# Attention with six head slots in place of five, loads a unit ahead, shared tail tiles and an earlier division of the last unit but one

## The chip, the cores and the metric

The kernel runs on one core of one Trainium2 chip. The metric is the device time of one execution in microseconds (us); the time given for a kernel is the median of its runs.

## The reference

The input `x` (2048 tokens, 576 wide) is layer-normed. Branch A is sliding-window attention with 32 heads of width 18 and a window of 256 keys; branch B is a gated MLP whose gate mixes tokens with a 2048 x 2048 matrix. The output is `x + A * silu(B)`.

```python
xn = layernorm(x)
q, k, v = heads(xn @ wqkv)                        # 32 heads of 18
p = softmax(where(0 <= i - j < 256, q @ k.T * 18**-0.5, -1e9))
s = merge(p @ v) @ wo
z = gelu(xn @ w_in); z1, z2 = z[:, :2304], layernorm(z[:, 2304:])
g = silu((z1 * (w_sp @ z2 + b_sp[:, None])) @ w_out)
out = x + s * g
```

## The kernel before

Products are formed in float32r with each operand split into a high and a low part (`hi, lo`), so that one product is three matmuls. The stages follow each other: q and k (stored in DRAM as `st_d`), v, z2, then **attention, with the z1 projection laid in between**, then the product with `wo` (L1148, tiles `wops`), then the token mixing (L1389) and the output (L1482).

**Attention.** A unit is four heads and one half of the tokens: `UNITS` holds 16 of them, units 0 to 7 for the first half and 8 to 15 for the second. A unit's heads come in two pairs; pair `p` is unit `p // 2`, heads `2a` and `2a + 1` with `a = p % 2`. A pair lies in one *slot*, a tile `att0` to `att4` of 128 x 2304 (q in the first 1024 columns, k behind it), the two heads in partitions 0 to 63 and 64 to 127. Pair `p` uses slot `p % NSLOT` (`q_of`, `k_of`). In orders without buffer numbers the slots read `att_2227` (slot 0), `att_2228` (1), `att_2229` (2), `att_6846` (3), `att_6848` (4) and, after the change, `att_6850` (5).

- `pair_jobs` (L547) loads a pair by eight DMAs from `st_d`. `open_unit(u)` puts the loads of pairs `2u + 3` and `2u + 4` on the planner's clock, 400 ns apart, as soon as all scores of unit `u - 1` have been handed out.
- `max_item` (L597 on TensorE, tile `sp`; L601 on VectorE) finds each query's maximum; 32 items make a unit. `max_split` and `max_end` (L610 to L623) split and turn the maxima, and four small DMAs `att<-mhl` (L627) put them into rows 54 and 55 of the slots.
- `scores` (L721, tile `tps`) makes scores less maximum, ScalarE takes the exponential (L725, `pt<-tps`), GpSimd clears what lies outside the band (L733, L736), and `pv` multiplies with v (L749, tile `ops`, a single PSUM buffer). v comes with a column of ones, so that each head's sum comes out as a row too.
- After half of a unit, and after the whole, ScalarE moves `ops` into `ou` (L764). There are two `ou` buffers: unit `u` writes into the one of unit `u - 2`, after that unit's stores `o_d<-ou` (L800). The last unit has a tile of its own, `oul`.
- `finish(u)` sets the division: `den<-ou` (L811), reciprocal (L784) at `INVERT_AT`, through DRAM (`r_d`, L786) back as `rp` (L791) at `FETCH_AT`, four multiplications on GpSimd (L795) and four stores (L800) at the times of `DIVIDE_AT`, counted from the end of the unit. For the last unit the same steps stand in the list `last` and run in the stage behind.
- `z1_rows(r)` is the fill: 972 matmuls for each half of the array (rows 0 to 63 write `ma`, rows 64 to 127 write `mb`, L668), 54 to a block of 128 features. `load_z1` fetches a block's weights into `z1raw` (L637), one buffer. A block's weights are fetched when the half that is behind enters the block before, and split on ScalarE and GpSimd (L683, `z1wh`, `z1wl`) from when *either* half is in the second bank of that block before.

**What sets the order.** A planner in the kernel keeps a clock per half of the array, with a fixed cost for each operation, and hands out at each step a score, a maximum, a fill matmul or a batch of `pv`. A maximum may be handed out when the planner's clock has passed the pair's last load by `LOAD_NS` (5500). All DMAs are issued by SyncE (SP), whose queue runs in the order that the planner gives; so do the queues of the four engines.

**Behind attention**, `wo_load(t)` loads 256 tokens of the heads' output from `o_d` (L973, L975; `t % 3` chooses `spare`, slot 0 or slot 1), `wo_split` (L1134 on ScalarE, L1135 and L1136 on VectorE) splits them into `ohl0`, `ohl1`, `ohl2`, and two halves of 28 matmuls (L1148) each make 128 tokens, moved out as `so` (L1181). `ohl0` lies where the `ou` and `rp` buffers of attention were.

Of the kernel before, what the change touches and what calls it, by code (L numbers as in the profile page):

```python
# [9 lines left out]
F32 = mybir.dt.float32  # L10
# [6 lines left out]
P = 128  # L17
# [19 lines left out]
NSLOT = 5  # L37
# [8 lines left out]
KEEP_NS = 1200  # L46
INVERT_AT = 9000
# [10 lines left out]
def f32(ap):  # L58
    return ap.bitcast(F32)
# [3 lines left out]
def kernel(  # L63
# [169 lines left out]
    with ExitStack() as early:  # L233
# [283 lines left out]
        with ExitStack() as ph:  # L517
# [37 lines left out]
            def after(ns, fn):  # L555
                waiting.append((clock + ns, fn))
# [182 lines left out]
            def pv(u, kb, qa, qz):  # L739
# [17 lines left out]
                if kb == 4 * c + 3:  # L757
                    if c % 2 == 0:
                        while parts.get(u - 2):
                            part(u - 2)  # L760
                        ous[u] = (ap_.tile([P, HS], F32, name="ou", bufs=2) if u < NU - 1 else
                                  aa.tile([P, HS], F32, name="oul", bufs=1))
                    ou = ous[u]
                    act.activation(ou[:, c % 2 * 512:c % 2 * 512 + 512], o_ps.pop(c), AF.Copy)  # L764
                    free_at = use("act", 500, 120)
                    for t in later:
                        t[0] = free_at
                    if c % 2 == 1:
                        finish(u, ou)
# [7 lines left out]
            def finish(u, ou):  # L777
# [5 lines left out]
                def invert():  # L783
                    dve.reciprocal(den, den)  # L784
                    t = use("dve", 270) - clock + 300
                    after(t + 1500, lambda: sp.dma_start(r_d[u].rearrange("h (a b) -> (h a) b", b=HS // 32), den))  # L786
                    for i in range(4):
                        after(t + FETCH_AT + 400 * i, partial(sums, i))
# [21 lines left out]
                else:  # L810
                    after(busy["act"] - clock + 1000, lambda: sp.dma_start(den, ou[DH::32, :]))  # L811
                    after(INVERT_AT, invert)
                    parts[u] = [partial(divide, a) for a in range(4)] + [partial(store, i) for i in range(4)]
                    for ns in DIVIDE_AT:
                        after(ns, partial(part, u))
# [153 lines left out]
            def wo_load(t):  # L969
                ts_ = slice(t * 2 * P, (t + 1) * 2 * P)  # L970
                home = (spare, slots[0], slots[1])[t % 3]
                raw = f32(home[:, :10 * P]).rearrange("p (k c) -> p k c", k=5)
# [3 lines left out]
                return raw  # L976

# [13 lines left out]
            spare = ab.tile([P, 10 * P], F32R, name="spare")  # L991
            with ExitStack() as heads:
# [22 lines left out]
                def open_unit(u):  # L1015

                    jobs = [(p, it) for p in (2 * u + 3, 2 * u + 4) if p < 2 * NU for it in [pair_jobs(p)]
                            for _ in range(8)]
                    for i, (p, it) in enumerate(jobs):
                        ns = 300 + 400 * i + (4000 if u == 0 else 0)  # L1020
# [538 lines left out]
```

## Time and profile before

| | us |
|---|---|
| median of 3 runs (1927.2 to 1933.6) | 1932.25 |
| the profiled execution | 1929.15 |
| its span | 1927.4 |
| attention with the fill | about 428 to 935 of the span |
| product with `wo` | about 942 to 1003 |

The span runs from the first to the last instruction; 1.75 us of the execution lie around it. PE is TensorE's matmuls, PEld its weight loads, DVE VectorE, ACT ScalarE, POOL GpSimd; SPq is SyncE, which issues the DMAs. PEclk is the share of TensorE's full clock that was granted. In a row of a timeline, what stands in brackets is the idle time before the instruction and what ended it.

### The profile page before, as it was taken

How to read it: one execution, taken by the hardware profiler on the slowest of the kernel's cores; microseconds unless marked ns; L12 is line 12 of the kernel's file. 1: busy time of each engine (PE TensorE's matmuls, PEld its weight loads, DVE VectorE, ACT ScalarE, POOL GpSimd, SP SyncE). 2: the span in 40 equal slices, each digit the busy share in tenths (PEclk: the TensorE clock that was granted, in tenths of full speed). 3: DMA queues.
4: the chain of work that ended last, by engine and by line, in shares of the span. 5: the costliest groups of instructions: out<-in, count | busy, mean ns of one | idle time of the engine just before them, and what ended most of it. 6: DMA issues, size and time to landing. Idle time of an engine off the chain costs nothing.

```text
span 1927.4 us, 38537 instructions
## 1 busy us (share of the span) xinstructions
PE 1867.1 (97%) x14552; PEld 1619.2 (84%) x14552; DVE 1037.9 (54%) x2273; ACT 916.3 (48%) x1760; POOL 397.8 (21%) x486
## 2 busy tenths in 40 slices
PE   8999999999988999999899999999999999999999
PEld 8999999997666676677698888888888888899998
DVE  6320334466666555654227787747776667563222
ACT  5432223225565555666458575465554534442211
POOL 3232343343445454455200000000000000000000
PEclk9999999999999998999899999999999999999999
DMA  8895798875565555664678677766676656875441
GB/s 259 196 235 150 240 316 274 272 256 156 154 167 160 156 164 151 155 181 132 176 246 274 218 256 243 248 211 225 201 255 225 193 162 190 270 230 157 141 139 58
DMA packets 234314, 389.85 MB, mean 202 GB/s; under 512 B 51984, under 2 KB 145680, under 8 KB 234000
## 3 DMA queue, kind: packets, MB, share of 16 engines
q1 hardware_dynamic: 234128, 387.39, 65.2%
q8 instruction: 114, 1.87, 0.4%
q14 instruction: 72, 0.59, 0.1%
HBM read 274.74 MB, written 111.78 MB: 201 GB/s over the span
## 4 chain that ended last, share of the span: by engine, by line
PE 76%; DMA 11%; DVE 5%; SPq 4%; issue 2%; ACT 2%; POOL 0%; POOLq 0%; DVEq 0%; ACTq 0%
PE acc L1389 32%; PE po L1482 12%; PE mb L204 9%; PE ma L204 5%; PE ma L668 4%; DMA att<-st_d 3%; PE ops L749 3%; PE mb L668 3%; PE tps L721 2%; PE sp L597 2%; PE wops L1148 2%; SPq L360 2%; DMA z1raw<-in_w_z_dram 2%; DMA st_d<-qkhl 1%; DMA rp<-r_d 1%
## 5 line engine op out<-in xcount | busy, mean ns | idle before, releaser
L1389 PE MATMUL acc<-spl,zh 128*128 128x512 f32 x1008 | 392.6, 390 | 0.9 <-DVE spl L114 0.5
L1389 PE MATMUL acc<-sph,zh 128*128 128x512 f32 x1008 | 392.2, 389 | 0.0
L1389 PE MATMUL acc<-sph,zl 128*128 128x512 f32 x1008 | 392.2, 389 | 0.0
L601 DVE CUSTOM_DVE_ANT_0 junk<-sp,band 128x384 bf16<-128x384 f32 (+1 forms) x512 | 276.3, 540 | 187.3 <-PE sp L597 101.3
L725 ACT ACTIVATE pt<-tps 128x384 f32<-128x384 f32 (+2 forms) x576 | 230.2, 439 | 145.4 <-PE tps L721 88.6
L668 PE MATMUL mb<-b,z1wh 64*128 64x512 f32 x648 | 228.4, 407 | 0.3 <-ACT z1o L673 0.2
L668 PE MATMUL ma<-b,z1wh 64*128 64x512 f32 x648 | 227.9, 407 | 0.5 <-ACT zt L943 0.4
L1389 PEld LDWEIGHTS acc<-spl,zh 128*128 128x128 f32 x1008 | 189.2, 188 | 41.6 <-DVE spl L114 2.6
L114 DVE TENSOR_TENSOR spl<-spr,sph 128x1024 fp32r<-128x1024 f32 x168 | 205.4, 1223 | 32.6 <-ACT sph L113 32.1
L1389 PEld LDWEIGHTS acc<-sph,zh 128*128 128x128 f32 x1008 | 189.2, 188 | 39.6
L1389 PEld LDWEIGHTS acc<-sph,zl 128*128 128x128 f32 x1008 | 189.2, 188 | 39.1
L113 ACT ACTIVATE zh<-b 128x384 fp32r<-128x384 f32 x168 | 87.5, 521 | 230.2 <-PE acc L1389 230.1
L721 PE MATMUL tps<-att 56*128 56x384 f32 (+1 forms) x576 | 180.0, 354 | 9.6 <-ACT pt L725 6.2
L597 PE MATMUL sp<-att 54*128 54x384 f32 (+1 forms) x512 | 161.0, 356 | 18.1 <-DMA att<-st_d 16.4
L113 ACT ACTIVATE sph<-spr 128x1024 fp32r<-128x1024 f32 x168 | 175.9, 1047 | 2.0 <-DMA spr<-in_w_sp_dram 1.7
L114 DVE TENSOR_TENSOR zl<-b,zh 128x384 fp32r<-128x384 f32 x168 | 93.2, 555 | 146.9 <-ACT zh L113 141.7
L1482 PE MATMUL po<-b,yh 128*128 128x288 f32 x840 | 147.1, 295 | 0.5 <-ACT gs L1469 0.5
L721 PEld LDWEIGHTS tps<-att 56*128 56x128 f32 x576 | 99.9, 188 | 42.6 <-ACT pt L725 18.0
L668 PE MATMUL mb<-b,z1wl 64*128 64x512 f32 x324 | 130.1, 402 | 0.0
L668 PE MATMUL ma<-b,z1wl 64*128 64x512 f32 x324 | 129.8, 401 | 0.0
L668 PEld LDWEIGHTS ma<-b,z1wh 64*128 64x128 f32 x648 | 119.6, 190 | 8.1 <-issue 2.5
L1482 PEld LDWEIGHTS po<-b,yh 128*128 128x128 f32 x840 | 124.2, 188 | 0.7 <-ACT gs L1469 0.7
(232 smaller groups left out, 4170.0 us busy)
## 6 DMA issues: line engine op xcount, KB each, us to landing
spr<-sc_d SPq DMA_DIRECT2D x96, 512.0 KB
spr<-in_w_sp_dram SPq DMA_DIRECT2D x72, 512.0 KB
zr<-z_d SPq DMA_DIRECT2D x144, 192.0 KB
z_d<-zt SPq DMA_DIRECT2D x48, 384.0 KB
z_d<-z1o SPq DMA_DIRECT2D x72, 256.0 KB
z1t<-z_d SPq DMA_DIRECT2D x72, 256.0 KB
y_d<-z1t SPq DMA_DIRECT2D x72, 256.0 KB
a<-in_w_sp_dram SPq DMA_DIRECT2D x64, 256.0 KB
```

What stands on the lines that cost most here:

```text
L113: act.activation(hi, src, AF.Copy)
L114: dve.tensor_tensor(lo, src, f32(hi), ALU.subtract)
L204: pe.matmul(banks[h][:, :n], *both[h][i], start=i == 0, stop=i == STEPS - 1)
L360: sp.dma_start(rows[c].rearrange("i h a p -> (i h) a p"), f32(hl[64 * n:64 * n + 64, c]).rearrange("q (a p) -> q a p", a=2))
L597: pe.matmul(ps[:, :w], q_of(u, j)[0:54, i * P:(i + 1) * P], k_of(u, j)[0:54, k0:k0 + w], start=True, stop=True)
L601: dve.tensor_tensor_reduce(out=junk[:, :w], in0=ps[:, :w], in1=band[:, m0:m0 + w], scale=1.0, scalar=-3.0e38, op0=ALU.add, op1=ALU.max, ac ...
L668: pe.matmul(ps, w, x_, start=n == 0, stop=n == STEPS - 1)
L721: pe.matmul(ps[:, :m * P], k_of(u, j)[:, (kb - base) * P:(kb - base + 1) * P], q_of(u, j)[:, (a - lo) * P:(a - lo + m) * P], start=True, s ...
L725: act.activation(pt[:, j, d0:d0 + n * P], ps[:, (qa - a) * P:(qa - a + n) * P], AF.Exp, scale=scale)
L749: pe.matmul(o_ps[c][32 * j:32 * j + 32, (qa - 4 * c) * P:(hi - 4 * c + 1) * P], vgs[u][:, kb - k0, j * VW:j * VW + 32], pt[:, j, (qa - kb) ...
L1389: pe.matmul(acc[j], z[:, ps], w[:, cs], start=s == i == 0 and n in OPENS, stop=s == 7 and i == 2, skip_group_check=True)
L1482: pe.matmul(po[i][:, a, :288], y if ahead else y[:, i * P:(i + 1) * P], w[a], start=f == 0 and m == 0, stop=f == NF - 1 and m == 2)
```

## The change

Pairs now have six slots. `open_unit(u)` loads pairs `2u + 4` and `2u + 5`, both of unit `u + 2`, 700 ns apart (unit 0 loads pairs 3, 4 and 5). The tiles `oul` and `spare` are gone: the last unit's output and the loads of `wo_load` with `t % 3 == 0` share a tile that takes the sixth slot's place when its last pair is done (`tail()`, shown as `att_14580`). The last unit but one inverts 4500 ns after its end in place of 9000, fetches `rp` 4500 ns behind that in place of 7500, and divides and stores 9500 ns earlier than `DIVIDE_AT` says.

```diff
--- before.py
+++ after.py
@@ -34,7 +34,7 @@
 UNITS = [(g, half) for half in range(2) for g in range(8)]
 NU = len(UNITS)
 MM = 227.0
-NSLOT = 5
+NSLOT = 6
 ZRB = 6
 WCB = 2
 RMN = 16
@@ -44,6 +44,7 @@
 LOAD_NS = 5500
 MAX_NS = 5000
 KEEP_NS = 1200
+LOAD_STEP = 700
 INVERT_AT = 9000
 FETCH_AT = 7500
 DIVIDE_AT = (22500, 24000, 25500, 27000, 31000, 31500, 32000, 32500)
@@ -759,7 +760,7 @@
                         while parts.get(u - 2):
                             part(u - 2)
                         ous[u] = (ap_.tile([P, HS], F32, name="ou", bufs=2) if u < NU - 1 else
-                                  aa.tile([P, HS], F32, name="oul", bufs=1))
+                                  tail()[:, 0:HS])
                     ou = ous[u]
                     act.activation(ou[:, c % 2 * 512:c % 2 * 512 + 512], o_ps.pop(c), AF.Copy)
                     free_at = use("act", 500, 120)
@@ -783,9 +784,9 @@
                 def invert():
                     dve.reciprocal(den, den)
                     t = use("dve", 270) - clock + 300
-                    after(t + 1500, lambda: sp.dma_start(r_d[u].rearrange("h (a b) -> (h a) b", b=HS // 32), den))
+                    after(t + (1500 if u < NU - 2 else 300), lambda: sp.dma_start(r_d[u].rearrange("h (a b) -> (h a) b", b=HS // 32), den))
                     for i in range(4):
-                        after(t + FETCH_AT + 400 * i, partial(sums, i))
+                        after(t + (FETCH_AT if u < NU - 2 else 4500) + 400 * i, partial(sums, i))
 
                 def sums(i):
                     sp.dma_start(rp[32 * i:32 * i + 32, :], r_d[u][i:i + 1, :].to_broadcast([32, HS]))
@@ -809,10 +810,11 @@
                                  lambda: [store(i) for i in range(4)]])
                 else:
                     after(busy["act"] - clock + 1000, lambda: sp.dma_start(den, ou[DH::32, :]))
-                    after(INVERT_AT, invert)
+                    sooner = 14000 if u == NU - 2 else 0
+                    after(max(INVERT_AT - sooner, 4500), invert)
                     parts[u] = [partial(divide, a) for a in range(4)] + [partial(store, i) for i in range(4)]
                     for ns in DIVIDE_AT:
-                        after(ns, partial(part, u))
+                        after(ns - sooner + (4500 if sooner else 0), partial(part, u))
 
             def sp_combos(stack):
 
@@ -968,13 +970,20 @@
 
             def wo_load(t):
                 ts_ = slice(t * 2 * P, (t + 1) * 2 * P)
-                home = (spare, slots[0], slots[1])[t % 3]
-                raw = f32(home[:, :10 * P]).rearrange("p (k c) -> p k c", k=5)
+                home = tail()[:, HS:] if t % 3 == 0 else f32(slots[t % 3 - 1][:, :10 * P])
+                raw = home.rearrange("p (k c) -> p k c", k=5)
                 sp.dma_start(raw[:, 0:4], o_d[0:512, ts_].rearrange("(k p) c -> p k c", p=P))
                 for a in range(2):
                     sp.dma_start(raw[64 * a:64 * a + 64, 4], o_d[512:576, ts_])
                 return raw
 
+            tails = []
+
+            def tail():
+                if not tails:
+                    tails.append(ab.tile([P, SLOT], F32, name="att5"))
+                return tails[0]
+
             def wow(i, k):
                 m = 5 * i + k
                 return slots[2 + m // 4][:, (HS if m > 7 else 0) + m % 4 * D:(HS if m > 7 else 0) + (m % 4 + 1) * D]
@@ -988,7 +997,6 @@
             for i in range(3, NSLOT):
                 slots.append(ab.tile([P, SLOT], F32R, name=f"att{i}"))
                 clear(i)
-            spare = ab.tile([P, 10 * P], F32R, name="spare")
             with ExitStack() as heads:
                 order.close()
                 heads.enter_context(tc.manual_schedule(engines=ENGINES | {ET.Activation, ET.SP}))
@@ -1014,10 +1022,10 @@
 
                 def open_unit(u):
 
-                    jobs = [(p, it) for p in (2 * u + 3, 2 * u + 4) if p < 2 * NU for it in [pair_jobs(p)]
-                            for _ in range(8)]
+                    pairs = (2 * u + 4, 2 * u + 5) if u else (3, 4, 5)
+                    jobs = [(p, it) for p in pairs if p < 2 * NU for it in [pair_jobs(p)] for _ in range(8)]
                     for i, (p, it) in enumerate(jobs):
-                        ns = 300 + 400 * i + (4000 if u == 0 else 0)
+                        ns = 300 + LOAD_STEP * i + (4000 if u == 0 else 0)
                         after(ns, partial(next, it, None))
                         head_ready[p] = clock + ns + LOAD_NS
 
```

Every engine carries out the same instructions as before (GpSimd one `memset` more, to clear the sixth slot); the order of attention is planned anew. Line numbers of the changed kernel are one to eight higher.

**Loads and stores on SP, around the opening of unit 5.** Before: the last load of pair 13 (slot 3), pair 14 (slot 4), and what follows up to the stores of unit 3.

```order
L547 DMA att_6846<-st_d 36x1024
L547 DMA att_6848<-st_d 36x1024
L547 DMA att_6848<-st_d 18x1024 x2
L547 DMA att_6848<-st_d 36x1024 x2
L547 DMA att_6848<-st_d 18x1024 x2
L547 DMA att_6848<-st_d 36x1024
L811 DMA den<-ou 128x1x32
L570 DMA z_d<-z1o 128x2x256
L637 DMA z1raw<-in_w_z_dram 128x1152
L570 DMA z_d<-z1o 128x2x256
L696 DMA vg<-v_d 128x8x89
L800 DMA o_d<-ou 18x1024 x4
```

The same place after the change: the loads of pair 15 (slot 3), up to the same stores.

```order
L571 DMA z_d<-z1o 128x2x256
L548 DMA att_6846<-st_d 36x1024
L548 DMA att_6846<-st_d 18x1024 x2
L548 DMA att_6846<-st_d 36x1024 x2
L548 DMA att_6846<-st_d 18x1024
L812 DMA den<-ou 128x1x32
L548 DMA att_6846<-st_d 18x1024
L697 DMA vg<-v_d 128x8x89
L548 DMA att_6846<-st_d 36x1024
L801 DMA o_d<-ou 18x1024 x4
```

Before, pair 13 was loaded here first, for maxima that TensorE takes 13 fill matmuls of a half behind unit 5's first score; now pairs 14 and 15 are, for maxima 31 behind that score and in unit 6, and pair 13 came a unit earlier. The stores of unit 3 stood five instructions behind the last load; now they stand directly behind it.

**The fill's weights on ScalarE, block 12 of the fill.** The last row is the first split of those weights; they are fetched at the eviction that ends block 10 in the half that is behind, here `ma`. Before, it is the `z1o<-ma` two rows ahead of the split:

```order
L764 ACTIVATE ou<-ops 128x512
L725 ACTIVATE pt<-tps 128x384 x3
L725 ACTIVATE pt<-tps 128x256 x4
L725 ACTIVATE pt<-tps 128x128 x4
L673 ACTIVATE z1o<-ma 128x512
L673 ACTIVATE z1o<-mb 128x512
L683 ACTIVATE z1wh<-z1raw 128x384
```

After, it is the first row:

```order
L674 ACTIVATE z1o<-ma 128x512
L726 ACTIVATE pt<-tps 128x128 x4
L726 ACTIVATE pt<-tps 128x256 x4
L726 ACTIVATE pt<-tps 128x384
L765 ACTIVATE ou<-ops 128x512
L726 ACTIVATE pt<-tps 128x384 x11
L674 ACTIVATE z1o<-ma 128x512
L674 ACTIVATE z1o<-mb 128x512
L726 ACTIVATE pt<-tps 128x384 x2
L684 ACTIVATE z1wh<-z1raw 128x384
```

One ScalarE instruction stood between the eviction and the split, now 25 do. For blocks 10 to 17 it was 1 to 15, now 15 to 27; for blocks 2 to 9 it was 20 to 27, now 16 to 27. The two halves of the array have drifted apart less: where unit 14 begins, 849 fill matmuls of `ma` and 864 of `mb` have been issued before, 815 and 816 now.

**SP behind the last unit.** Before, from the last evictions of the fill on:

```order
L570 DMA z_d<-z1o 128x2x256 x2
L973 DMA att_2227<-o_d 128x4x256
L975 DMA att_2227<-o_d 64x256 x2
L973 DMA att_2228<-o_d 128x4x256
L975 DMA att_2228<-o_d 64x256 x2
L807 DMA den<-oul 128x1x32
L800 DMA o_d<-ou 18x1024 x4
L147 DMA zr<-z_d 128x384 x4
L805 DMA r_d<-den 128x32
```

After, from the last unit's `den` on (the stores `o_d<-ou` of unit 14 stand ahead of these rows):

```order
L808 DMA den<-att_14580 128x1x32
L148 DMA zr<-z_d 128x384 x4
L806 DMA r_d<-den 128x32
L975 DMA att_14580<-o_d 128x4x256
L977 DMA att_14580<-o_d 64x256 x2
L148 DMA zr<-z_d 128x384
L792 DMA att_6848<-r_d 32x1024 x4
L1118 DMA z_d<-z1o 128x2x256
L148 DMA zr<-z_d 128x384
L1118 DMA z_d<-z1o 128x2x256
L975 DMA att_2227<-o_d 128x4x256
L977 DMA att_2227<-o_d 64x256 x2
```

The stores of unit 14 moved ahead of the last unit's `den`; the loads into slots 0 and 1 moved from ahead of `den` to behind the last unit's fetch of sums and the last two stores of the fill. On TensorE, 43 matmuls of the fill (19 `ma`, 24 `mb`) now stand between the last `ops` and the first `wops`; before, none did.

## Prediction

> **What bounds the kernel now.** I read the table by stage first (columns: stretch and length in us; busy us and instructions of PE, PEld, DVE, ACT and POOL; granted clock, DMA share, GB/s). The change touches these three stretches.
>
> ```profile
> 428.00:660.00 232.00, 209.48 (x1934) 160.62 (x1934) 140.79 (x530) 130.45 (x309) 105.24 (x153) 0.97 0.60 162
> 660.00:936.00 276.00, 260.27 (x2492) 191.73 (x2490) 147.71 (x510) 172.21 (x433) 135.24 (x200) 0.98 0.58 159
> 936.00:1004.00 68.00, 60.79 (x439) 60.04 (x440) 16.55 (x19) 29.26 (x40) 4.79 (x4) 0.93 0.71 223
> ```
>
> TensorE idles there for 22.5, 15.7 and 7.2 us; the other engines are busy for under two thirds, and TensorE's work stays the same. So what can be won is its idle time and the clock lost with it. The waits of TensorE from 428 to 970 us say what ends the idle time (total us, times, longest):
>
> ```profile
> PE sp L597 <- DMA att<-st_d: 16.4, 10, 4.0
> PE wops L1148 <- ACT ohl L1134: 7.7, 2, 7.4
> PE tps L721 <- ACT pt L725: 6.2, 4, 3.9
> PE ops L749 <- ACT ou L764: 5.3, 4, 1.5
> PE tps L721 <- DMA att<-mhl: 3.1, 1, 3.1
> PE ops L749 <- POOL pt L736: 2.1, 1, 2.1
> ```
>
> The clock drops to 0.50 in whole windows, and those of these stages follow waits (columns of the first table):
>
> ```profile
> 444.25:447.66 3.41, 3.41 (x19) 2.71 (x17) 1.56 (x6) 2.83 (x5) 0.00 (x0) 0.50 0.76 209
> 621.74:628.57 6.83, 6.06 (x31) 5.86 (x32) 2.35 (x9) 2.34 (x5) 1.94 (x4) 0.50 0.82 204
> 655.87:659.28 3.41, 3.41 (x19) 2.77 (x20) 1.70 (x6) 0.99 (x2) 3.12 (x5) 0.50 0.77 201
> 724.14:727.55 3.41, 3.41 (x21) 3.14 (x18) 1.89 (x8) 2.29 (x5) 2.30 (x4) 0.50 0.72 179
> 751.45:758.27 6.82, 5.55 (x37) 3.90 (x39) 0.00 (x0) 3.65 (x11) 0.64 (x1) 0.50 0.73 222
> 935.76:946.00 10.24, 3.59 (x14) 3.31 (x14) 3.50 (x5) 2.43 (x2) 1.51 (x3) 0.50 0.61 190
> ```
>
> Half of TensorE's busy time in such a window is lost. Each term below is a wait and its window.
>
> **A: loads a unit ahead.** The pair waited for is the first that is loaded in the unit. From the timeline, the three waits that have a window behind them:
>
> ```profile
> 622.51 0.55 PE L597 MATMUL sp<-att 54*128 54x256 f32 x1 [2.38 <-DMA att<-st_d]
> 655.73 0.59 PE L597 MATMUL sp<-att 54*128 54x384 f32 x2 [3.99 <-DMA att<-st_d]
> 723.32 0.44 PE L597 MATMUL sp<-att 54*128 54x384 f32 x2 [1.72 <-DMA att<-st_d]
> ```
>
> After the change the second pair of each opening has a whole unit before its maxima. The first pair is still used in the unit of its load, but 26 to 31 fill matmuls of a half behind the unit's first score in units 0 to 7, and 18 to 24 in the later ones. Before, the first pair loaded stood 8 to 13 behind in the first units, and 6 to 22 in the later ones, where few waits were left. Ten waits are 16.4; I leave 3 (pair 3, and one or two late in the stage): **-13.4** (bounds 0 and -16.4). The windows lost (6.06 + 3.41 + 3.41) / 2 = 6.4; I leave 1: **-5.4** (0 to -6.4). The loads, now 700 ns apart, and the one `memset` more cost nothing: they lie beside a whole unit of fill; without that cover the loads would cost the waits above again.
>
> **B: the first maxima.** SP took 5 us over four small moves, behind six loads, and unit 0's first scores waited for them:
>
> ```profile
> 437.23 5.01 SPq L627 DMA_DIRECT2D att<-mhl  x4
> 443.92 0.45 PE L721 MATMUL tps<-att 56*128 56x384 f32 x2 [3.07 <-DMA att<-mhl]
> ```
>
> Four loads stand ahead of the last move now. I take half of the wait and the window of 3.41 / 2: **-3** (0 to -4.8).
>
> **C: the fill's weights.** ScalarE waits in its queue for `z1raw`, so the exponentials behind it are late, and TensorE with them:
>
> ```profile
> 751.98 0.52 ACT L683 ACTIVATE z1wh<-z1raw 128x384 fp32r<-128x384 f32 x1 [5.59 <-DMA z1raw<-in_w_z_dram]
> 752.72 0.74 PE L721 MATMUL tps<-att 56*128 56x256 f32 x2 [3.90 <-ACT pt L725]
> 786.38 0.38 PE L721 MATMUL tps<-att 56*128 56x256 f32 x1 [1.79 <-ACT pt L725]
> ```
>
> The fetch itself, the longest of the chain of waits:
>
> ```profile
> 778.49 7.13 DMA z1raw<-in_w_z_dram
> ```
>
> This is the place that the order of block 12 shows: one ScalarE instruction between fetch and split before, 25 now, 15 at the least for a block of the second half. ScalarE carries out one per 0.64 us there (433 in 276 us), so 15 are 9.6 us, more than the 7.1 of a fetch. I count 3.9 + 1.8 and GpSimd's 2.1, which ends 4 us behind the second, and 5.55 / 2 of clock: 10.6. Waits at other places of a new order can stand in for one: **-8.5** (0 to -10.6).
>
> **D: the `ou` buffers, a loss.** Unit `u` is evicted only when the stores of unit `u - 2` have landed. One such store in the chain, and then two evictions, of units 2 and 6:
>
> ```profile
> 512.78 4.22 DMA o_d<-ou
> ```
>
> ```profile
> 517.19 0.60 ACT L764 ACTIVATE ou<-ops 128x512 f32<-128x512 f32 x1 [1.66 <-DMA o_d<-ou]
> 627.78 1.27 SPq L800 DMA_DIRECT2D o_d<-ou  x2
> 635.48 0.60 ACT L764 ACTIVATE ou<-ops 128x512 f32<-128x512 f32 x1 [0.27 <-PE ops L749]
> ```
>
> Units 2 to 5 wait, 5.3 in all on TensorE; unit 6 has 2 us to spare (629.05 + 4.22 against 635.5). `DIVIDE_AT` still counts from the end of unit `u - 2`, while the unit and a half up to the eviction shrinks by what A removes, some 1.5 x 2 us, and the stores now stand straight behind the loads. So each of the four waits grows by 0 to 3, I say 1.5: 6 us. Queued behind the eviction on ScalarE are exponentials, behind the one `ops` buffer the rest of `pv`. A wait of 1.7 had a window behind it; three waits that pass it lose 3.41 / 2 each: **+11** (0 to +22: six units by 2 and a window each).
>
> **E: the sooner division of unit 14.** Its four multiplications move from behind the selects of unit 15 to between them, and now wait for `rp` there, whose last fetch has the first load from `o_d` ahead of it. GpSimd's waits for `rp`:
>
> ```profile
> POOL ou L795 <- DMA rp<-r_d: 10.2, 4, 5.1
> ```
>
> The mean is 2.5; a select queued behind makes `pv` late by as much: **+2.5** (0 to +5.1). The reciprocal, `r_d`, four fetches and four stores are issued as before, and lie beside fill.
>
> **F: the end of attention.** From the last long `pv` to the first `wops`, TensorE is busy for 3.11 of 11.4 us (a stretch, columns as above; then a step of the fill; then the chain's longest DMA there; then the timeline):
>
> ```profile
> 930.97:942.41 11.44, 3.11 (x35) 1.02 (x35) 0.02 (x1) 3.31 (x8) 4.01 (x6) 0.71 0.68 214
> ```
>
> ```profile
> 926.46 0.39 PE L668 MATMUL ma<-b,z1wh 64*128 64x512 f32 x1
> 926.69 0.39 PE L668 MATMUL ma<-b,z1wh 64*128 64x512 f32 x1
> ```
>
> ```profile
> 934.71 5.37 DMA att<-o_d
> ```
>
> ```profile
> 932.73 0.68 SPq L973 DMA_DIRECT2D att<-o_d  x1
> 941.09 1.27 ACT L1134 ACTIVATE ohl<-spare 128x1280 fp32r<-128x1280 f32 x1 [5.42 <-DMA o_d<-ou]
> 942.41 24.39 PE L1148 MATMUL wops<-att,ohl 128*128 128x288 f32 x168 [7.40 <-ACT ohl L1134]
> 944.49 0.32 SPq L805 DMA_DIRECT2D r_d<-den  x1
> 947.21 1.76 SPq L791 DMA_DIRECT2D att<-r_d  x4
> 948.24 0.65 ACT L1181 ACTIVATE so<-wops 128x576 f32<-128x576 f32 x1 [4.72 <-PE wops L1148]
> 951.91 0.65 ACT L1181 ACTIVATE so<-wops 128x576 f32<-128x576 f32 x1 [2.43 <-PE wops L1148]
> ```
>
> `ohl0` waited for unit 14's stores, whose memory it takes. These now land while the fill still runs: 43 of its matmuls stand behind the last `ops`, 24 steps of 0.23, 5.5 us. They cover the last exponentials (3 us of the thin stretch go, 0 to 4), and the wait of 7.4 goes with the 2 us that the first half lost to the clock (5.8 up to 948.2, then 3.7 to 951.9). **Late next is the second tile, `ohl1`**, since the order has put its load behind `r_d`, the sums and two stores. From `ohl0` done, by these rows: 2.1 to `r_d` (942.4 to 944.5), 2.7 to the sums, 1.8 for them, 1.3 for three more DMAs at their 0.4, 1.9 to issue three (932.7 to 934.6), 5.4 to land, 1.3 to split: 16.5. `ohl0` is done some 2.5 behind the last `ops`, `ohl1` at 19, and the first two halves at 5.5 + 2 x 3.7 = 12.9. That is a new wait of 6, with 2 of clock; queued behind `ohl1` on ScalarE are evictions, which three buffers cover. 8 for 9.4, less the 3: **-4.4** (-12.4 with no new wait, +3).
>
> **The sum.** -13.4 - 5.4 - 3 - 8.5 + 11 + 2.5 - 4.4 = -21.2 from the profiled 1929.15 is 1908. The median of the runs lies 3 above that execution; for it I predict **1908.5**.
>
> **Rivals.** *The stores take it all back (slower).* SP holds the stores behind sixteen loads as it held the moves at 437.23, 5 us longer. D is then six units by 5 more and a window each, 46 in place of 11: 1943. It decides from 3.5 us more per unit, where the sum is zero. The order speaks for it; against it, loads 700 ns apart leave SP and its DMAs more room.
>
> The Trainium skill, "DMA: Bandwidth & Descriptors", section "Queues, rings and completion order", says that a DMA's completion lands only after every earlier write of the DMA engines it runs on. By that alone a store straight behind a load lands with the load, 5.4 us in place of 4.2, D would be +18, and the time 1916; no row of before has a store there, so it stays open.
>
> *Loads stay late.* If the first pair of each later unit waits as those of the first units do now, about 1.6 (16.4 over ten), 10 more of A stay and 5 of clock: 1924.
>
> *Nothing is won.* The waits are ends of a chain that moves along: ScalarE or VectorE would be late by as much. Against it: they are busy for 62% and 61% at most by the first table. 1929, give or take 4.
>
> **How the numbers follow.** The forecast gets 0.62 (1896 to 1920, the terms by half their bounds), late loads 0.12, nothing won 0.13, the stores 0.13. 1895 to 1931 leaves out the slow case and some of the edges. A measurement of this kernel tells 0.3%, 5.8 us, from no change. Faster: the forecast and most of the late loads, 0.73; same 0.14; slower 0.13.
>
> **What would show it.** A: hardly a wait of L597 for `st_d` in units 0 to 7. C: no wait of L683 over 2 us. D: `ou` waits of 2 to 4 us in units 2 to 5. F: the first `wops` without a wait, and one of 6 us ahead of the third half. The forecast is wrong if `ou` waits pass 7 us, or if TensorE still idles over 30 us from 428 to its last `ops`.

## The result, and the profile after

The changed kernel takes 1907.87 us (median of 4 runs, 1904.54 to 1910.25) against 1929.72 for the kernel before on the same chip: a ratio of 0.9885, 95% interval 0.9856 to 0.9914. The forecast was 1908.5, in 1895 to 1931. The profiled execution is 1909.97, its span 1908.2, so 19.2 less than before by the spans. Line numbers of the changed kernel are 1 to 8 higher than before (L597 is L598, L764 is L765, L1148 is L1156).

TensorE's waits from 428 to 970 us, columns as in the prediction:

```profile
PE ops L750 <- ACT ou L765: 11.5, 5, 4.7
PE ops L750 <- POOL pt L737: 8.6, 7, 2.0
PE wops L1156 <- ACT ohl L1142: 6.2, 1, 6.2
PE tps L722 <- DMA att<-mhl: 1.8, 1, 1.8
```

The wait for `st_d`, first before with 16.4, is gone, and so is ScalarE's `pt`, 6.2. The wait for `ou` has grown from 5.3 to 11.5, and **GpSimd's `pt` from 2.1 to 8.6**. ScalarE's waits for the fill's weights, which C is about, before and after:

```profile
ACT z1wh L683 <- DMA z1raw<-in_w_z_dram: 12.5, 5, 5.6
```

```profile
ACT z1wh L684 <- DMA z1raw<-in_w_z_dram: 2.2, 1, 2.2
```

By stage (columns as in the prediction), from the first scores to the end of `pv` and fill, and from there to the last `wops`; first the kernel before, then the changed one:

```profile
444.00:935.00 491.00, 456.97 (x4327) 341.40 (x4327) 279.01 (x1001) 297.81 (x731) 234.07 (x345) 0.98 0.58 158
935.00:1005.46 70.46, 62.26 (x450) 61.50 (x450) 16.55 (x19) 29.86 (x41) 5.79 (x6) 0.93 0.72 228
```

```profile
444.00:918.16 474.16, 451.65 (x4328) 339.66 (x4328) 278.06 (x1004) 300.50 (x732) 236.34 (x349) 0.97 0.62 164
918.16:986.43 68.27, 62.07 (x449) 61.55 (x450) 13.32 (x16) 28.65 (x40) 2.49 (x2) 0.95 0.72 232
```

Attention is 16.8 shorter and the product with `wo` 2.2; what follows takes 922.0 before and 921.8 after. In attention, 11.5 of the 16.8 is idle time (34.0 to 22.5) and 5.3 is busy time with the same matmuls (what is known of it stands in the account of the prediction). It is not clock: there are as many half-clock windows as before, at other places (the five of before up to 758 held 21.8 us of TensorE's work; the first five here hold 22.7):

```profile
444.39:447.80 3.41, 3.29 (x19) 2.57 (x17) 1.13 (x4) 2.81 (x5) 0.00 (x0) 0.50 0.87 246
516.08:522.91 6.83, 6.24 (x45) 5.08 (x45) 2.66 (x11) 3.36 (x9) 1.22 (x2) 0.50 0.02 5
546.79:550.20 3.41, 3.37 (x26) 2.53 (x28) 1.06 (x4) 1.51 (x4) 0.56 (x1) 0.50 0.00 0
625.30:632.13 6.83, 6.34 (x34) 4.71 (x36) 2.92 (x10) 2.19 (x5) 2.83 (x5) 0.50 0.93 243
799.38:802.79 3.41, 3.41 (x20) 3.24 (x17) 1.83 (x8) 1.64 (x4) 1.97 (x4) 0.50 1.08 208
929.09:935.92 6.83, 3.91 (x15) 3.63 (x16) 2.75 (x3) 4.70 (x6) 0.00 (x0) 0.50 0.38 117
```

The timeline of TensorE names the wait at each of them but the first, which follows the wait of 1.8 for the moves of the maxima (`mhl`). Two are `ou`, two are GpSimd's selects, the last is the third half of `wops`:

```profile
516.67 0.66 PE L750 MATMUL ops<-pt,vg 128*32 128x128 f32 x8 [4.24 <-ACT ou L765]
546.83 0.44 PE L750 MATMUL ops<-pt,vg 128*32 128x128 f32 x4 [4.70 <-ACT ou L765]
625.79 0.87 PE L750 MATMUL ops<-pt,vg 128*32 128x384 f32 x4 [1.71 <-POOL pt L737]
798.30 0.43 PE L750 MATMUL ops<-pt,vg 128*32 128x128 f32 x8 [2.03 <-POOL pt L737]
932.01 1.33 PE L1156 MATMUL wops<-att,ohl 128*128 128x288 f32 x4 [6.20 <-ACT ohl L1142]
```

**Behind the two `ou` waits** are the stores of units 0 and 1. SP's and ScalarE's rows (the first `o_d<-ou` is all four stores of unit 0, the second the last two of unit 1; `ou<-ops` are the evictions of units 2 and 3 that wait for them):

```profile
509.58 1.42 SPq L801 DMA_DIRECT2D o_d<-ou  x4
516.02 0.60 ACT L765 ACTIVATE ou<-ops 128x512 f32<-128x512 f32 x1 [4.98 <-DMA o_d<-ou]
540.27 0.69 SPq L801 DMA_DIRECT2D o_d<-ou  x2
546.18 0.60 ACT L765 ACTIVATE ou<-ops 128x512 f32<-128x512 f32 x1 [5.26 <-DMA o_d<-ou]
```

From the end of the last store's issue to the eviction it is 5.0 (511.00 to 516.02) and 5.2 (540.96 to 546.18). Measured in the same way, the four evictions that waited before came 3.6 to 4.3 behind their stores (the first from 513.1 to 517.19). So a store took 0.9 and 1.7 longer to land, while the waits of the two evictions grew by 3.3 and 3.2; the rest, 2.4 and 1.6, is that the stores were issued later, as seen from the eviction. The rule of the Trainium skill in the prediction (a store straight behind a load would land with it) is not decided by these rows: unit 3's stores stand behind loads as well, and unit 5's eviction came 4.0 behind them (597.29 to 601.31). Its price for the six units, 18, did not come, since only two of them waited long.

**Behind GpSimd's waits** are the four multiplications of a unit. GpSimd's rows up to the wait at 625.79:

```profile
618.63 0.74 POOL L796 TENSOR_TENSOR ou<-ou,rp 128x256 f32<-128x256 f32 x1 [5.85 <-DMA rp<-r_d]
619.33 1.02 POOL L684 TENSOR_TENSOR z1wl<-z1raw,z1wh 128x384 fp32r<-128x384 f32 x1
620.30 0.74 POOL L796 TENSOR_TENSOR ou<-ou,rp 128x256 f32<-128x256 f32 x1
621.00 1.00 POOL L684 TENSOR_TENSOR z1wl<-z1raw,z1wh 128x384 fp32r<-128x384 f32 x1
621.97 0.63 POOL L734 TENSOR_SCALAR_AFFINE_SELECT pt<-pt 128x512 f32<-128x512 f32 x1
622.55 0.63 POOL L737 TENSOR_SCALAR_AFFINE_SELECT pt<-pt 128x512 f32<-128x512 f32 x1
623.15 1.41 POOL L796 TENSOR_TENSOR ou<-ou,rp 128x256 f32<-128x256 f32 x2
624.52 0.62 POOL L734 TENSOR_SCALAR_AFFINE_SELECT pt<-pt 128x512 f32<-128x512 f32 x1
625.11 0.62 POOL L737 TENSOR_SCALAR_AFFINE_SELECT pt<-pt 128x512 f32<-128x512 f32 x1
```

`rp` holds the reciprocal sums that a unit's output is multiplied with. The first multiplication waits 5.85 for it, and from 618.63 to 625.73 GpSimd has no pause: six pieces of division and split and four selects in one go, and `pv` waits for the last select.

### The profile page after: what moved, and what is told of

Same layout as the page of the kernel before. It is cut to its first block, busy times and chain, and to the rows that moved or that the text cites. A ratio compares the mean times of both kernels' runs of the same rounds, so it can differ in the third digit from the quotient of the medians.

```text
span 1908.2 us, 38517 instructions
## 1 busy us (share of the span) xinstructions
PE 1862.0 (98%) x14552; PEld 1623.7 (85%) x14552; DVE 1033.3 (54%) x2273; ACT 917.0 (48%) x1760; POOL 397.5 (21%) x487
## 4 chain that ended last, share of the span: by engine, by line
PE 84%; DMA 6%; DVE 4%; ACT 2%; SPq 2%; issue 1%; POOL 1%; ACTq 0%; DVEq 0%; POOLq 0%
PE acc L1397 34%; PE po L1490 12%; PE mb L205 11%; PE ma L669 6%; PE mb L669 4%; PE ma L205 4%; PE ops L750 4%; PE wops L1156 3%; PE tps L722 2%; PE sp L598 2%; DMA st_d<-qkhl 2%; DMA att<-st_d 1%; SPq L361 1%; DMA rp<-r_d 1%; DMA o_d<-ou 1%
## 5 line engine op out<-in xcount | busy, mean ns | idle before, releaser
L598 PE MATMUL sp<-att 54*128 54x384 f32 (+1 forms) x512 | 162.8, 356 | 1.7 <-DVE mx L602 1.5
L722 PEld LDWEIGHTS tps<-att 56*128 56x128 f32 x576 | 101.0, 189 | 33.5 <-issue 12.9
```

Source lines behind the costliest of these rows:

```text
L598: pe.matmul(ps[:, :w], q_of(u, j)[0:54, i * P:(i + 1) * P], k_of(u, j)[0:54, k0:k0 + w], start=True, stop=True)
L722: pe.matmul(ps[:, :m * P], k_of(u, j)[:, (kb - base) * P:(kb - base + 1) * P], q_of(u, j)[:, (a - lo) * P:(a - lo + m) * P], start=True, s ...
```

## The experiments

Theory: the loads a unit ahead remove the waits for `st_d` and, by the order that comes with them, those for `z1raw`; `ou` takes part of it back, and the sooner division is worth little. Rivals: the sixth slot alone, or the sooner division, carries the gain. All ratios are against the kernel before on the same chip; its medians there were 1929.1 to 1929.7. The differences in the text are of medians, and the runs stood on several chips: by the ratios stores_sooner would be 8.9 faster than the changed kernel in place of 11.2, wo_early 0.8 in place of 3.4, and no_sooner 2.1 slower in place of 0.0.

| run | median us | ratio, 95% interval |
|---|---|---|
| changed kernel | 1907.87 | 0.9885 (0.9856 to 0.9914) |
| loads_as_before | 1925.92 | 0.9984 (0.9970 to 0.9999) |
| sooner_alone | 1928.58 | 0.9996 (0.9983 to 1.0008) |
| no_sooner | 1907.88 | 0.9896 (0.9868 to 0.9924) |
| fetch_sooner | 1923.53 | 0.9967 (0.9952 to 0.9982) |
| divide_early | 1896.17 | 0.9829 (0.9804 to 0.9854) |
| stores_sooner | 1896.72 | 0.9839 (0.9822 to 0.9856) |
| rp_sooner | 1903.52 | 0.9861 (0.9846 to 0.9875) |
| stores_only | 1902.39 | 0.9859 (0.9843 to 0.9876) |
| wo_early | 1904.52 | 0.9881 (0.9858 to 0.9903) |
| step400 | 1912.20 | 0.9898 (0.9878 to 0.9918) |
| best1 | 1882.05 | 0.9758 (0.9738 to 0.9778) |
| best2 | 1880.74 | 0.9740 (0.9724 to 0.9757) |

### Is it the loads or the slot?

```diff
-LOAD_STEP = 700
+LOAD_STEP = 400
...
-                    pairs = (2 * u + 4, 2 * u + 5) if u else (3, 4, 5)
+                    pairs = (2 * u + 3, 2 * u + 4)
```

> The changed kernel with six slots, shared tail tiles and the sooner division, but each opening loads pairs 2u+3 and 2u+4, 400 ns apart, as in the kernel before. My theory (term A: it is the loads a whole unit ahead that remove the waits): waits of the maxima for st_d come back, 10 to 16 us with 5 of clock, and a part of the ou waits (11.5 now) goes, since the units are longer: 1916 to 1924. Rival, the sixth slot alone removes them, since a load no longer meets a slot that was only just released: waits for st_d under 4 us, 1906 to 1911.

18 us slower than the changed kernel, 3 us faster than before. TensorE's waits of this run, as above:

```profile
PE sp L598 <- DMA att<-st_d: 14.8, 7, 4.6
PE tps L722 <- ACT pt L726: 6.9, 5, 3.1
PE ops L750 <- ACT ou L765: 4.3, 3, 2.0
```

A sixth slot without the loads ahead is worth nearly nothing. Not only the waits for `st_d` are back: so is ScalarE's `pt`, and `ou` is as small as before. All three hang on the loads' place. Since the planner reckons with the loads, the order of every engine changes with them; what the earlier DMAs do and what the new order does is not told apart by this run.

### The sooner division

On the kernel before, the edit to `invert` and `finish` alone (sooner_alone); on the changed kernel, that edit undone (no_sooner, shown here).

```diff
-                    after(t + (1500 if u < NU - 2 else 300), lambda: sp.dma_start(r_d[u].rearrange("h (a b) -> (h a) b", b=HS // 32), den))
+                    after(t + 1500, lambda: sp.dma_start(r_d[u].rearrange("h (a b) -> (h a) b", b=HS // 32), den))
...
-                        after(t + (FETCH_AT if u < NU - 2 else 4500) + 400 * i, partial(sums, i))
+                        after(t + FETCH_AT + 400 * i, partial(sums, i))
...
-                    sooner = 14000 if u == NU - 2 else 0
-                    after(max(INVERT_AT - sooner, 4500), invert)
+                    sooner = 0
+                    after(INVERT_AT, invert)
```

> The kernel before with five slots and its loads, and the sooner inversion, fetch and division of unit 14 alone. My theory (E and F): about 2 us faster than before, 1926 to 1929, the wait ahead of the first wops gone and a new one at the third half. Rival 1, the sooner division carries most of the change: 1920 or below. Rival 2: slower than before, since the four multiplications now stand between the selects of unit 15: 1932 or above.

> The changed kernel, but unit 14 is inverted, fetched and divided at the same times as the other units. My theory (terms E and F of the prediction): the first tile ohl0 waits again for unit 14's stores, TensorE waits some 7 us ahead of the first wops and the window behind it runs at half clock, while the wait of 6.2 ahead of the third half goes; the waits for unit 14's selects (about 1.2 us) go too. In all 3 to 5 us slower than the changed kernel, about 1912. Rival 1, the sooner division carries most of the change: 10 us or more slower, 1918 or above. Rival 2, it is worth nothing: within 2 us of 1908.

Neither makes a difference that can be told: 0.6 us and 0.0. The trace of no_sooner shows why (its rows of `wops` that waited):

```profile
914.47 25.19 PE L1156 MATMUL wops<-att,ohl 128*128 128x288 f32 x168 [3.53 <-ACT ohl L1142]
941.75 0.78 PE L1156 MATMUL wops<-att,ohl 128*128 128x288 f32 x4 [2.09 <-ACT ohl L1142]
```

The first half waits again, 3.5, and the seventh 2.1; the wait of 6.2 ahead of the third is gone. 5.6 stands for 6.2: the sooner division mostly moves the wait. In these single traces the stretch from the last `ops` to the last `wops` is a little shorter with it (75.5 in no_sooner, 74.1 in the changed kernel; 70.5 before, 67.4 in sooner_alone). That confirms the exchange which F describes; the 3 to 5 us that I expected the medians do not show, though intervals of over 5 us to either side do not exclude them.

### Term C by itself

On the kernel before, the weights of a fill block are fetched when the half that is ahead enters the block before. Every engine but SP keeps its order.

```diff
...
+                            b or n or f + 1 == FH // P or f + 1 in z1got or fetch_z1(f + 1)
                             if f + 1 < FH // P and min(z1_at) == f:
...
+            def fetch_z1(f):
+                z1got.add(f)
+                z1raws[f] = zw.tile([P, 9, P], F32, name="z1raw", bufs=1)
+                sp.dma_start(z1raws[f], w_z1[f])
```

> The kernel before with five slots and its loads, and one edit: a block's fill weights are fetched when the leading half enters the block before, in place of the trailing half. All engines but SP keep their order. My theory (term C): ScalarE no longer waits for z1raw, TensorE's waits for pt at about 752 and 786 go, with the window of 6.8 at half clock between them: 6 to 10 us faster than before, 1919 to 1923. Rival, the time saved is given back at the next load of a pair, since the waits for st_d are ends of a chain that moves along: waits for st_d grow from 16 to 20 or more, 1926 to 1930.

6 us faster than before (3.5 to 9.3 by the interval), where C said 8.5. TensorE's waits of this run (scores and exponentials are L727 and L731 here):

```profile
PE sp L597 <- DMA att<-st_d: 15.1, 10, 3.8
PE tps L727 <- ACT pt L731: 1.0, 3, 0.4
```

ScalarE's waits for `z1raw` fall from 12.5 to 3.6 and TensorE's for ScalarE's `pt` from 6.2 to 1.0. The waits for `st_d` do not grow: the gain is not handed on to the next load.

### The `ou` buffers and the division of the early units

First the whole division of units 0 to 5 came 3500 ns sooner.

```diff
+                    early = 3500 if u < 6 else 0
-                    after(max(INVERT_AT - sooner, 4500), invert)
+                    after(max(INVERT_AT - sooner, 4500) - early, invert)
...
-                        after(ns - sooner + (4500 if sooner else 0), partial(part, u))
+                        after(ns - sooner + (4500 if sooner else 0) - early, partial(part, u))
```

> The changed kernel, with the inversion, fetch, division and stores of units 0 to 5 all 3500 ns earlier. My theory (term D: the ou waits of units 2 and 3 are stores of units 0 and 1 that are issued too late behind sixteen loads): waits for ou under 2 us in place of 11.5, the two windows behind them at full clock (5 us): 12 to 15 us faster than the changed kernel, 1893 to 1897. Rival 1, the stores are held up by SP's loads wherever they stand: the ou waits stay at 8 us or more, 1905 to 1909. Rival 2, the earlier multiplications on GpSimd hold up the selects instead (waits of pv for pt on GpSimd from 8.6 to 15 or more): gain under 5 us, 1903 or above.

12 us faster than the changed kernel, as expected, but not for the reason given: `ou` still waits 7.2 in all, where under 2 was expected. The planner reckons with the division's time on GpSimd, and the order of every engine is another in this run; it cannot carry term D. It also has a wait of its own, since the inversion now comes before its data (VectorE's row, then TensorE's):

```profile
487.22 0.35 DVE L785 RECIPROCAL den<-den 128x32 f32<-128x32 f32 x1 [5.75 <-DMA den<-ou]
```

```profile
488.04 0.68 PE L598 MATMUL sp<-att 54*128 54x384 f32 x1 [4.25 <-DVE mx L602]
```

So three runs followed that move DMAs in SP's queue and leave the order of VectorE, ScalarE and GpSimd as it was: the fetches of `rp` 1500 ns sooner (rp_sooner, the first edit), the stores 3500 ns sooner (stores_only, the second), and both (stores_sooner), for units 0 to 5.

```diff
-                        after(t + (FETCH_AT if u < NU - 2 else 4500) + 400 * i, partial(sums, i))
+                        after(t + ((FETCH_AT - (1500 if u < 6 else 0)) if u < NU - 2 else 4500) + 400 * i, partial(sums, i))
...
-                    for ns in DIVIDE_AT:
+                    for ns in DIVIDE_AT[:4] + tuple(t - (3500 if u < 6 else 0) for t in DIVIDE_AT[4:]):
```

> The changed kernel, and on SP alone the stores of units 0 to 5 come 3500 ns sooner and the fetches of their rp 1500 ns sooner; all other engines keep their order. My theory (term D: evictions wait for stores that SP issues too late): the ou wait of unit 2 (4.2) goes, that of unit 3 (4.7) shrinks by 1 to 3, a window or two at half clock goes with them: 6 to 10 us faster than the changed kernel, 1898 to 1902. Rival 1, the stores land no sooner because they now stand among the loads: ou waits stay at 10 or more, 1905 to 1910. Rival 2, the loads that the stores push back make the maxima wait: waits for st_d of 3 us or more, 1904 or above.

> The changed kernel, and on SP alone the fetches of rp of units 0 to 5 come 1500 ns sooner, the stores stay; all other engines keep their order. My theory on the new waits of pv for pt on GpSimd (8.6, not in the prediction): the selects stand behind multiplications that wait for rp. Then these waits fall to about 4 as in stores_sooner, a window of 6.8 at half clock at about 625 goes, and the ou waits stay at 10 or more: 4 to 8 us faster than the changed kernel, 1900 to 1904. Rival, the selects are late for another reason (ScalarE's exponentials): GpSimd's waits stay at 8, 1906 to 1909.

> The changed kernel, and on SP alone the stores of units 0 to 5 come 3500 ns sooner, the fetches of rp stay; all other engines keep their order. Theory (term D by itself): the ou wait of unit 2 falls from 4.2 to about 1, that of unit 3 stays near 4 since its stores already stand right behind their multiplications, GpSimd's waits stay at 8: 3 to 7 us faster than the changed kernel, 1901 to 1905, and with rp_sooner the two gains make about the 11 of stores_sooner. Rival, the stores are worth nothing without the sooner multiplications: 1906 to 1909.

Both: 11.2 us faster than the changed kernel. By themselves, 4.4 and 5.5: together 9.9, nearly the whole, though the interval of each overlaps that of the changed kernel, and only the run with both just touches it. The waits tell which is which. Of rp_sooner, of stores_only, of stores_sooner:

```profile
PE ops L750 <- ACT ou L765: 12.2, 6, 5.1
PE ops L750 <- POOL pt L737: 3.5, 4, 1.2
```

```profile
PE ops L750 <- ACT ou L765: 9.5, 5, 4.8
PE ops L750 <- POOL pt L737: 7.4, 7, 1.8
```

```profile
PE ops L750 <- ACT ou L765: 8.0, 5, 4.4
PE ops L750 <- POOL pt L737: 4.1, 4, 1.7
```

Earlier `rp` takes GpSimd's waits from 8.6 to 3.5 and leaves `ou`; earlier stores take `ou` from 11.5 to 9.5 (unit 2 alone: 4.2 to 2.1, where about 1 was expected) and leave GpSimd's. And the two windows behind GpSimd's waits go with `rp`: the same stretches in rp_sooner have a clock of 1.00 (0.83 and 0.89 in the changed kernel).

```profile
612.00:632.00 20.00, 18.13 (x188) 13.13 (x188) 12.55 (x47) 12.21 (x28) 11.15 (x17) 1.00 0.85 216
790.00:806.00 16.00, 14.54 (x141) 11.06 (x143) 10.02 (x36) 11.58 (x28) 8.92 (x14) 1.00 0.79 174
```

The second stretch lies behind units 0 to 5, whose fetches alone were moved, so not all of it is the edit's own: its wait is 2.03 in the changed kernel and 1.2 here. Of the 5.1 that GpSimd's waits fell by, the three waits at 570, 623 and 626, where fetches were moved, are 3.7. The `ou` wait of unit 3 stays (4.75 in stores_only, 4.40 in stores_sooner): the stores that it waits for, those of unit 1, already stand right behind their multiplications. That only an earlier multiplication could move them is not tested by itself.

### The load of `ohl1`

```diff
+                oraws += [wo_load(t) for t in range(1, 3)]
                 for ns in (3000, 100000):
...
-                    if ns == 3000:
-                        oraws += [wo_load(t) for t in range(1, 3)]
```

> The changed kernel, with the second and third loads of heads' output (tiles ohl1 and ohl2) handed to SP ahead of the last fill stores and of the last unit's division; all other engines keep their order. My theory (term F: the wait of 6.2 ahead of the third half is the load's place in SP's queue): no wait over 1 us of wops for ohl, the window of 6.8 at about 929 at full clock: 5 to 9 us faster than the changed kernel, 1899 to 1903. Rival, the loads wait for the two slots of the last unit and hold up SP, so that the wait turns up at the last unit's division, at zr or at the fill's stores: 1906 to 1910.

The median is 3.4 lower, which its interval does not tell from nothing. The wait at the third half goes, as F's account of SP's queue has it, and the seventh half waits instead, as in no_sooner (the last row; ahead of it ScalarE's, where the split for that half stands behind an eviction that waits for a store):

```profile
939.13 0.65 ACT L1188 ACTIVATE so<-wops 128x576 f32<-128x576 f32 x1 [9.34 <-DMA s_d<-so]
939.68 1.26 ACT L1141 ACTIVATE ohl<-att 128x1280 fp32r<-128x1280 f32 x1
```

```profile
940.99 0.79 PE L1155 MATMUL wops<-att,ohl 128*128 128x288 f32 x4 [2.03 <-ACT ohl L1141]
```

So the place in the queue is shown to be the cause of that wait (with one thing more: ScalarE's split of `ohl1` now stands ahead of the last two evictions of the fill). Of its 6.2 and 2 of clock the trace gives back 3.8 from the last `ops` to the last `wops` (74.1 to 70.2), and the medians 3.4 at best. The wait of 2.0 at the seventh half, with a window of 3.41 at half clock behind it, is most of what is missing.

### Denser loads

```diff
-LOAD_STEP = 700
+LOAD_STEP = 400
```

> The changed kernel with the loads 400 ns apart in place of 700. My theory: the loads have a whole unit either way, no waits for st_d, and the ou waits hang on the times of the division, not on the loads: within 4 us of the changed kernel, 1904 to 1912. Rival (the prediction's slow case, in which SP holds small moves and stores behind a block of loads): denser loads hold the moves of the maxima and the stores longer, waits for mhl and ou grow, 1914 or above.

4.3 above the changed kernel, not told apart by the intervals, and just above the 1912 that I gave as the upper end. No wait for `st_d`, `ou` 10.1, GpSimd's `pt` 9.8, `mhl` 2.7: the slow rival, SP held by a block of loads, does not come with denser loads either.

### The two together

best1 has the division of units 0 to 5 sooner but the inversion at its time, and the loads of wo_early; best2 also drops the sooner division of unit 14.

```diff
-                        after(t + (FETCH_AT if u < NU - 2 else 4500) + 400 * i, partial(sums, i))
+                        after(t + (FETCH_AT - (3500 if u < 6 else 0) if u < NU - 2 else 4500) + 400 * i, partial(sums, i))
...
+                    early = 3500 if u < 6 else 0
...
-                        after(ns - sooner + (4500 if sooner else 0), partial(part, u))
+                        after(ns - sooner + (4500 if sooner else 0) - early, partial(part, u))
...
```

> The changed kernel, with the fetch, division and stores of units 0 to 5 3500 ns earlier and the inversion left at its time (so that VectorE does not wait for den), and the two loads of heads' output sooner. My theory: the waits that divide_early still has, 4.25 for VectorE with a window of 6.8 and 3.0 ahead of wops with one of 3.4, go; from 1896 that makes 1884 to 1890. Rival, the planner lays the units otherwise and the waits come back as others (ou, pt on GpSimd): 1893 to 1900.

> The kernel best1 (1882) with unit 14's sooner division undone. My theory: in best1 a select of unit 15 waits 4.7 us behind a multiplication that waits for rp (with a window of 6.8 at half clock), and 25 us of fill stand behind the last pv, which cover unit 14's stores; so the sooner division is a loss there: 4 to 8 us faster than best1, 1874 to 1878. Rival, the tile ohl0 waits for those stores and the first wops with it: 1882 or above.

1882 and 1881: 26 and 27 us faster than the changed kernel, and best2 is 2.6% faster than before. best1 is below the 1884 to 1890 that I expected, best2 above its 1874 to 1878. The planner lays every engine's order anew in both, so these runs tell their time and not which part of the edit earned it. The last stage of best1 has TensorE busy all of it at full clock:

```profile
904.54:958.59 54.05, 54.05 (x406) 54.05 (x406) 11.67 (x14) 26.35 (x37) 0.00 (x0) 1.00 0.70 232
```

Behind its last `pv` the fill, with the first `wops` between, goes on for 25 us (879.6 to 904.5) and covers the loads of the first tiles. Its longest wait is the sooner division's own (GpSimd's row, then TensorE's; the load `att<-o_d` is no operand of the multiplication; the profile puts the wait down to the DMA that landed last):

```profile
866.38 0.72 POOL L796 TENSOR_TENSOR ou<-ou,rp 128x256 f32<-128x256 f32 x1 [8.76 <-DMA att<-o_d]
```

```profile
867.74 0.66 PE L750 MATMUL ops<-pt,vg 128*32 128x128 f32 x8 [4.67 <-POOL pt L734]
```

In best2 it is gone and the first `wops` waits 2.8 instead: a trade again, 1.3 us between the two, which is nothing that can be told.

## Why the prediction was right, and where it was not

The sum of -21.2 met -19.2 by the profiles. The mechanism of its largest term is shown: undoing the loads ahead brings 14.8 us of waits for `st_d` back and, with all else that hangs on the loads' place, 18 us of time. The median of 1907.87 is closer to 1908.5 than the prediction earned: it says that the median lies 3 above the profiled execution and then adds half a microsecond; with four runs of each, the median lies 0.6 above it before and 2.1 below it after. By its steps:

- **A, waits:** -13.4 forecast, -16.4 found; the three that were left over did not come.
- **A, clock:** -5.4 forecast. The windows at 621, 655 and 724 went (6.4), but those at 516, 546, 625 and 799 came, and the windows of attention weigh the same as before (21.8 and 22.7 of work). The balance of the clock failed, not this term: D's +5 foresaw the first two of the new windows, no term the other two.
- **B:** half of the wait was right (3.1 to 1.8); its window stayed, so -1.3 for -3.
- **C:** alone it is worth 6 of the 8.5, within its bounds. TensorE's waits for ScalarE's `pt` are gone; one wait of ScalarE for `z1raw` is left, 2.2 where C's sign was none over 2. That "GpSimd's 2.1" goes with it was wrong; see the next but one.
- **D:** +11 forecast. `ou` has 6.2 more (6 forecast) and two windows, (6.24 + 3.37) / 2 = 4.8 (5 forecast). The size was right, the shape was not: two waits of 4 to 5 in units 2 and 3, in place of four of 2 to 4 in units 2 to 5. "No row of before has a store there" overlooked unit 8's stores at 757.08, 0.6 behind a load; nobody waited for them, so they would not have settled the rule.
- **The term that was missing:** GpSimd. E counted only unit 14's multiplications among selects (+2.5; 1.17 came at that place). But multiplications of other units wait for `rp` too, and the selects behind them are late: 6.5 more of waiting and (6.34 + 3.41) / 2 = 4.9 of clock, 11 in all. rp_sooner shows the cause for the units whose fetches it moved, 3.7 of the waits and the first window. The row "DMA rp<-r_d: 10.2, 4, 5.1" was there before, and I had read it for unit 14 alone; and it is not the whole, since the profile puts six more waits of these multiplications down to a load that they do not read:

```profile
POOL ou L795 <- DMA att<-st_d: 25.3, 6, 7.2
```

So the multiplications waited for more before (35.5 in all) than after (24.2), and it cost TensorE less. That selects now stand behind them with less slack is argued, not tested.

- **E and F:** together -1.9 forecast; undoing the sooner division changes nothing that can be told. The new wait of 6.2 stands where and as long as F said (6, third half, half clock behind it), and takes back most of what the first wait gave. The stage from the end of the fill to the last `wops` is 2.2 shorter. F's own stretch starts earlier, at the last long `pv`: from there it is 74.6 before (930.89 to 1005.46) and 76.6 after (909.84 to 986.43), with 6.8 of fill in it that stood ahead of it before, so 4.8 shorter by that estimate, near F's 4.4.

With the sizes found, A to F and the missing term make -16.4 - 6.4 - 1.3 - 6.2 - 2.8 + 11.0 + 11.4 - 2.2 = -12.9 (C by its waits and window here). The other 6, of which some 2.6 lie in F's own stretch, are nearly the 5.3 of shorter busy time in attention. By lines it is the fill: its matmuls, 1860 in both traces, keep TensorE busy for 324.5 before and 319.7 after, while scores are 1.8 shorter and maxima and `pv` 3.7 longer. For 86 us before, and 80 after, only one of the two halves of the array had a fill matmul; that fits halves that drift apart less, but no run tests it. So the sum held by luck: a loss of 11 that no term had was met by 4 more from A than forecast and by these 6.

Of the rivals, late loads are excluded by the missing waits for `st_d`, "nothing is won" by the time as well, and the slow one by D's size: 3.5 more per unit was its point; units 2 and 3 have 3.1 and 3.2 more, units 4 and 5 less than before. Of the two signs of a wrong forecast, no single `ou` wait passes 7 us (4.7 at most; 11.5 is their sum), and TensorE idles for under 25 us from 428 to its last `ops`, where 30 was the limit.

## What to carry to other kernels

Loading a stage further ahead pays by the waits that it removes, and then every step that is set by a fixed delay from the start of a unit comes late, since the unit is shorter: list these (inversion, fetch, division, store, next load) and move them with it; here that, the sooner load of `ohl1` and unit 14's division at its old time were worth about as much as the change itself (27 us, from 1908 to 1881, and 22). To test such a step, move only DMAs in the issuing queue and leave the order of the engines alone; a run in which the planner lays everything otherwise tells only its time. Before a moved wait is counted as won, look for the next one on the same chain: at the end of attention it turned up at another half of `wops` each time.

## What the runs showed of the hardware

Over the 14 profiles of these runs, from 428 to 970 us, all 47 waits of TensorE of 2.3 us or longer had a half-clock window at or within 3.5 us behind them; of 43 between 1.4 and 2.3 us, 25 had one. The shortest in the changed kernel that had one is the 1.71 at 625.79, with 6.83 us at 0.50. The Trainium skill, "TensorE: Matmul & The Clock Gate", section "HAM oscillation — how this bites in real kernels", warns of idle gaps over about 3.4 us; here gaps of half that length already cost a window as often as not. For a forecast, one window of 3.41 at half speed for each wait over 2 us is too little: of the 54 waits of 2 us or longer, 18 were followed by a window of 3.41, 29 by one of 6.83, four by one of 10.24 and three by none.
